# Batch 0's casts, copies and filler matmuls rearranged, and two loads of x split, in a cross-attention and MLP kernel

## The chip, the cores and the metric

One core of one Trainium2 chip. The metric is device time in microseconds (us), median over executions; a profile of one execution gives its span, the time from the first to the last recorded event. The measured time is about 1.8 us above the span of the same execution (213.31 and 211.5 for the profiled run of before).

## The reference, cut to what matters

```python
# x: (8, 8, 512, 64), state: (8, 8, 32, 64), w_in: (512, 2048), w_out: (2048, 512), float32
scores = 0.125 * x @ state.T                # per batch and head: 512 x 32
xread  = softmax(scores) @ state            # 512 x 64
scores2 = 0.125 * state @ x.T
sread  = softmax(scores2) @ x               # 32 x 64
h = concat([xread, sread]) as (4352, 512) @ w_in
out = (h * sigmoid(h)) @ w_out              # (4352, 512)
```

## The kernel before

The kernel multiplies state by w_in beforehand (the tile `W`, one per batch), so that softmax weights times `W` give `h` directly. Almost all of the time goes to two groups of full-width matmuls: G1 (`h`, from softmax weights and `W`) and G2 (`o`, from the activated `h` and w_out). Only batch 0 has nothing to hide behind; its softmax has to be made while the weights are still being loaded. The start, cut:

```python
# loads: x of batch 0 on SyncE in two halves; weights on GpSimd, in this order
load_w_in(0, 128); load_w_in(128, 384)
load_w_out(0, 2);  load_w_out(2, 2)
# ... state of batch 1
load_w_in(512)                              # third piece, columns 512 to 1023
load_w_out(4, 4)
# first half of x (heads 0-3): cast, transpose on TensorE, copy out of PSUM
cast_x(0, nc.vector, 0, 2, 0, 4)            # pieces c = 0, 1
cast_x(0, nc.scalar, 2, 2, 0, 4)            # pieces c = 2, 3
# ...
cast_x(0, nc.scalar, 2, 2, 4, 4)            # second half of x on three engines
cast_x(0, nc.gpsimd, 0, 1, 4, 4)
pe_transpose_x(0, 0, 2, new_o, (nc.vector, nc.vector))
cast_x(0, nc.vector, 1, 1, 4, 4)
# ... (keep_busy(n) is n filler matmuls on zeros)
scores(0, 0); exps(0, 0)
keep_busy(1, psH, "h1")
pe_transpose_x(0, 1, 2, new_h, both)
norm(0, 0)                                  # product on GpSimd
scores(0, 1, 2); exps(0, 1)
norm(0, 1, ((nc.vector, 0, 4),), 2)         # product on VectorE
w1_cols(0, [(0, 128)], (nc.scalar, nc.scalar))
# ... more loads
keep_busy(3, psH, "h1")
pss0 = w1_mms(0, [(128, 384)])              # needs the second piece of w_in
keep_busy(2, psH, "h1")
# attention-weight transposes (first half of heads, then second), their copies,
# G1 for ft = 0..3, G2 for ft = 0, 1, then
# w1_mms(0, [(512, 512)])                   # needs the third piece of w_in
```

In the profile before, every group of matmuls from there on has its inputs in time. Batches 4 to 7 load x on SyncE, 1 MB each, two batches ahead of the one that is being multiplied.

The softmax here doesn't subtract the row's maximum and nothing guards it: scores larger than these inputs give would overflow.

## Time and profile before

| | before |
|---|---|
| time, median of the first 3 runs | 212.74 us |
| its profiled execution | 213.31 us, span 211.5 us |
| TensorE busy | 96% of the span |
| 384-column group starts | 10.29 us, at the landing of its weights |
| 512-column group starts | 15.59 us, at the landing of its weights |
| from there to the end | 195.95 us |

A row of a timeline has the start, the length, engine, source line, operation, output and inputs, shape, count, and in brackets the idle time before it and who ended it. L469 is the multiplication of state by w_in (first a group of 128 columns, then 384, then 512), L398 the attention-weight transposes, L253 the transposes of x, L306 the scores, L165 filler, L525 is G1 and L566 G2. The chain of waits is the path that ended last: start, length, what.

### The profile page before, as it was taken

The numbers are of one execution on the slowest core, as the hardware profiler recorded it, in microseconds if no ns is written. First come the engines' busy times: TensorE is split into PE (matmuls) and PEld (weight loads), VectorE is DVE, ScalarE is ACT, GpSimd is POOL, SyncE is SP. The second block draws the span as 40 slices with busy tenths as digits, with TensorE's granted clock in tenths as the row PEclk, the third lists the DMA queues.
The fourth block names the chain that finished last, engine by engine and source line by source line (L and its number), as shares of the span: only waits on it lengthen the run. The fifth ranks groups of instructions, "written<-read, shape, count | busy, mean of one in ns | idle before, by whom it ended". The sixth has DMA issues, their size and how long they took to land.

```text
span 211.5 us, 3841 instructions
## 1 busy us (share of the span) xinstructions
PE 203.7 (96%) x1550; PEld 96.8 (46%) x1575; DVE 74.1 (35%) x146; ACT 139.3 (66%) x244; POOL 40.1 (19%) x62
## 2 busy tenths in 40 slices
PE   7799999999999999999999999999999999999993
PEld 2444454444444444444444444444444444466653
DVE  3842257657841236113410653043412306100011
ACT  3866677899577867697569855996775166644410
POOL 8672215503320042012201202000200000000000
PEclk9999999999999999999999999999999999999999
DMA  6999999995549756555935429114221111011112
GB/s 196 193 203 207 287 258 340 226 272 179 103 104 239 205 130 138 122 176 102 233 80 183 104 64 207 50 53 99 80 69 37 63 64 53 0 50 50 53 50 99
DMA packets 42929, 28.65 MB, mean 135 GB/s; under 512 B 28064, under 2 KB 37792, under 8 KB 42912
## 3 DMA queue, kind: packets, MB, share of 16 engines
q1 hardware_dynamic: 36720, 20.65, 37.4%
q0 software_dynamic: 5904, 7.64, 17.4%
q8 instruction: 12, 0.20, 0.4%
q10 hardware_dynamic: 288, 0.13, 0.2%
q14 instruction: 5, 0.04, 0.1%
HBM read 17.43 MB, written 8.91 MB: 125 GB/s over the span
## 4 chain that ended last, share of the span: by engine, by line
PE 90%; DMA 5%; POOL 2%; issue 1%; DVE 0%; POOLq 0%
PE o L566 50%; PE h L525 25%; DMA w_in_sb<-in_moe_w_in_dram 5%; PE ps_w L469 4%; PE h L546 3%; PE o_a L566 3%; PE o_part L588 2%; PE ps_sr L416 1%; PE ps_scT L332 1%; POOL w_in_sb L150 1%; POOL w_out_sb L153 1%; PE ps_sc L306 0%; PE ps_xt L253 0%; DVE W L159 0%; POOL st_n L191 0%
## 5 line engine op out<-in xcount | busy, mean ns | idle before, releaser
L566 PE MATMUL o<-w_out_sb,g 128*128 128x512 bf16 x480 | 129.5, 379 | 1.3 <-issue 0.5
L557 ACT ACTIVATE g<-h 128x512 bf16<-128x512 f32 (+1 forms) x143 | 81.3, 573 | 34.1 <-PE h L525 19.9
L566 PEld LDWEIGHTS <-g 128*128 128x128 bf16 x528 | 50.3, 98 | 59.1 <-issue 3.8
L525 PE MATMUL h<-aT,W 128*128 128x512 bf16 x247 | 73.1, 379 | 0.1
L159 DVE COPY o_sb<-o 128x512 f32<-128x512 f32 x15 | 10.4, 691 | 89.1 <-PE o L566 86.2
L525 PEld LDWEIGHTS <-W 128*128 128x128 bf16 x254 | 24.5, 98 | 30.3 <-issue 0.7
L159 DVE CAST W<-ps_w 128x512 bf16<-128x512 f32 (+2 forms) x36 | 22.2, 658 | 23.2 <-PE ps_w L469 23.2
L157 ACT ACTIVATE W<-ps_w 128x512 bf16<-128x512 f32 (+1 forms) x32 | 16.2, 562 | 11.1 <-PE ps_w L469 11.1
L159 POOL CAST x_nat<-x_f 128x512 bf16<-128x512 f32 x24 | 14.7, 655 | 35.7 <-DMA x_f<-in_x_dram 35.7
L157 ACT ACTIVATE o_sb<-o 128x512 f32<-128x512 f32 x16 | 9.5, 597 | 14.4 <-PE o L566 11.9
L362 POOL TENSOR_TENSOR an<-e,rcn 128x512 bf16<-128x512 bf16 x5 | 7.6, 1517 | 48.0 <-DVE rcn L360 48.0
L469 PE MATMUL ps_w<-w_in_sb,stT 64*32 64x512 bf16 (+2 forms) x264 | 10.3, 373 | 0.6 <-DMA w_in_sb<-in_moe_w_in_dram 0.6
L566 PE MATMUL o_a<-w_out_sb,g 128*128 128x512 bf16 x31 | 9.8, 379 | 0.2
L546 PE MATMUL h<-xmT,w_in_sb 128*128 128x256 bf16 x64 | 9.6, 273 | 0.1
L546 PEld LDWEIGHTS <-w_in_sb 128*128 128x128 bf16 x64 | 6.3, 98 | 3.9
L359 DVE TENSOR_REDUCE rs<-e 128x32 f32<-128x1024 bf16 x5 | 6.1, 1213 | 3.1 <-DMA e<-eT 3.1
L165 PE MATMUL ps_busy<-busy 128*128 128x512 bf16 x15 | 5.9, 497 | 1.2 <-DVE warm L172 1.2
L346 ACT ACTIVATE eT<-ps_scT 128x512 bf16<-128x512 f32 x10 | 5.4, 597 | 1.6 <-PE ps_scT L332 1.6
L786 ACT ACT_TABLE_LOAD x5 | 6.4, 1283 | 0.1
L469 PEld LDWEIGHTS <-stT 64*32 64x32 bf16 x264 | 3.2, 90 | 6.0 <-issue 4.1
L382 POOL TENSOR_TENSOR an<-exp_nat,rc 128x512 bf16<-128x512 bf16 x3 | 3.1, 1048 | 14.8 <-DVE rc L380 14.8
L768 ACT ACT_TABLE_LOAD x4 | 5.1, 1283 | 0.1
(76 smaller groups left out, 99.7 us busy)
## 6 DMA issues: line engine op xcount, KB each, us to landing
out_dram<-o_sb SPq DMA_DIRECT2D x33, 256.0 KB, 2.5
x_f<-in_x_dram SPq DMA_DIRECT2D x4, 1024.0 KB, 6.1
x_f<-in_x_dram POOLq DMA_DIRECT2D x2, 1024.0 KB, 11.9
w_in_sb<-in_moe_w_in_dram POOLq DMA_DIRECT2D x3, 512.0 KB, 10.5
x_f<-in_x_dram SPq DMA_DIRECT2D x2, 512.0 KB, 4.7
w_out_sb<-in_moe_w_out_dram POOLq DMA_DIRECT2D x4, 256.0 KB, 12.0
w_out_sb<-in_moe_w_out_dram POOLq DMA_DIRECT2D x2, 512.0 KB, 12.2
x_f<-in_x_dram POOLq DMA_DIRECT2D x2, 512.0 KB, 15.2
```

Of the source, the lines that this page charges most:

```text
L157: nc.scalar.activation(dst, src, func=COPY, bias=0.0)
L159: eng.tensor_copy(dst, src)
L165: nc.tensor.matmul(ps[:], busy[:, 0:128], busy[:], start=True, stop=True, skip_group_check=True)
L346: nc.scalar.activation(t[:, hg], scT_ps[hg][:], func=EXP, bias=0.0, scale=SCALE)
L359: nc.vector.tensor_reduce(rs[:], e2[b][:], axis=AX, op=ADD)
L362: eng.tensor_tensor(a[:, hg], e2[b][:, hg], rc[:, hg].to_broadcast([128, 4, 4, NS]), op=MULT)
L469: nc.tensor.matmul(pss[f, hg][ds(32 * s, 32), 0:n], stT[ds(r, 64), b, h // 2, s % 2, :], w_in_sb[ds(r, 64), h // 2, ds(f, n)], start=True, ...
L525: nc.tensor.matmul(h_ps[k][:], W1[b][:, hg, ds(128 * ft, 128)], aT[b][:, hg, :, :], start=(hg == 0), stop=(hg == 1), skip_group_check=True,)
L546: nc.tensor.matmul(ps[:, 0:256], w_in_sb[:, kt, ds(128 * ft, 128)], xmT[:, :, kt].rearrange("p t n b -> p t (n b)"), start=(kt == 0), stop ...
L557: nc.scalar.activation(g[:, 0:n], ps[:, 0:n], func=SILU, bias=0.0)
L566: nc.tensor.matmul(outs[tt][:], gt[b * NFT + ft][:, ds(128 * tt, 128)], w_out_sb[:, ft, :], start=(ft == 0), stop=(ft == NFT - 1), skip_gr ...
L786: nc.scalar.activation(warm[:], busy[:, 0:1], func=SILU, bias=0.0)
```

## The change

The intent: shorten the path from x to the first G1 by spreading casts and copies and by moving filler matmuls out of it, and make two later loads of x finer. The diff:

```diff
--- before.py
+++ after.py
@@ -257,7 +257,8 @@
                     )
             copy(engs[u], xT[b][:, ds(m * u, m), ds(2 * hg, 2), :], ps[:])
 
-    cast_x(0, nc.vector, 0, 2, 0, 4)
+    for c in (0, 1):
+        cast_x(0, nc.vector, c, 1, 0, 4)
     cast_x(0, nc.scalar, 2, 2, 0, 4)
     for u in range(2):
         copy(
@@ -267,10 +268,9 @@
         )
     o_tags = ["o0", "o1"]
     new_o = lambda sh, dt, nm: psO.tile(sh, dt, tag=o_tags.pop(), name=nm)
-    cast_x(0, nc.scalar, 2, 2, 4, 4)
-    cast_x(0, nc.gpsimd, 0, 1, 4, 4)
-    pe_transpose_x(0, 0, 2, new_o, (nc.vector, nc.vector))
-    cast_x(0, nc.vector, 1, 1, 4, 4)
+    pe_transpose_x(0, 0, 2, new_o, both)
+    for c in (0, 2):
+        cast_x(0, nc.vector, c, 2, 4, 4)
 
     st_x = pers.tile([128, 8, B, 4, 2, 2], BF16)
 
@@ -611,7 +611,6 @@
     keep_busy(1, psH, "h1")
     scores(0, 0)
     exps(0, 0)
-    keep_busy(1, psH, "h1")
     pe_transpose_x(0, 1, 2, new_h, both)
     norm(0, 0)
     scores(0, 1, 2)
@@ -630,11 +629,10 @@
     load_x(2)
     for i in (1, 2):
         ones_beside_x(i, nc.gpsimd)
-    keep_busy(3, psH, "h1")
+    keep_busy(5, psH, "h1")
     banks[:] = ["a2", "a3"]
     turn[0] = 0
     pss0 = w1_mms(0, [(128, 384)])
-    keep_busy(2, psH, "h1")
     for c in (0, 2):
         ps_a = (psO, psA)[c // 2].tile(
             [128, 2, 128], BF16, tag=("o1", "a0")[c // 2], name="ps_at"
@@ -768,7 +766,8 @@
                     nc.scalar.activation(warm[:], busy[:, 0:1], func=EXP, bias=0.0)
                 if m + 1 < B:
                     if at == (0, 2):
-                        load_x(m + 1, eng=nc.sync)
+                        for h in range(0, H, 4 if b < 3 else H):
+                            load_x(m + 1, h, 4 if b < 3 else H, nc.sync)
                     if at == (1, 0):
                         for c in range(4):
                             cast_x(m + 1, nc.gpsimd, c, 1)
```

Casts, copies and filler belong to batch 0; the last hunk splits the loads of batches 4 and 5 in halves of four heads.

## The prediction

> **What bounds the kernel now.** I read the page first (busy shares, slices), then the chain of work that ended last in order of time, then the timelines of TensorE, VectorE and ScalarE over the first 18 us, because every part of the change but one lies there.
>
> The page of the kernel before:
>
> ```profile
> span 211.5 us, 3841 instructions
> PE 203.7 (96%) x1550; PEld 96.8 (46%) x1575; DVE 74.1 (35%) x146; ACT 139.3 (66%) x244; POOL 40.1 (19%) x62
> ```
>
> TensorE is busy 96% of the time; the page's row of slices (5.3 us each) is thin only in the first two and the last. So a gain can come only from matmuls that go away or from the holes at the start. The change removes one matmul, and that one is filler. The chain of waits (columns: start, length, what) says which event the start hangs on:
>
> ```profile
> 1.61 1.63 POOL w_in_sb L150 x2
> ...
> 5.13 10.42 DMA w_in_sb<-in_moe_w_in_dram
> 15.55 0.04 issue
> 15.59 0.62 PE ps_w L469 x16
> ```
>
> Followed back from the end, everything is TensorE to 15.59 us; there the chain leaves TensorE for a transfer, the third piece of the weights w_in (512 columns), issued by GpSimd at 5.13 and landed at 15.55. Ahead of it stand only GpSimd's earlier issues. The casts, transposes and softmax of batch 0, which the change rearranges, are not on this chain at all. The TensorE timeline over the same stretch (start, length, line, operation, count, idle before and who ended it):
>
> ```profile
> 5.54 0.62 PE L253 MATMUL ps_xt<-ident,x_rows 128*128 128x128 bf16 x8 [0.45 <-DVE x_rows L159]
> 6.46 0.62 PE L306 MATMUL ps_sc<-stT,xT 128*128 128x64 bf16 x8
> 6.92 0.38 PE L165 MATMUL ps_busy<-busy 128*128 128x512 bf16 x1
> 7.13 0.67 PE L253 MATMUL ps_xt<-ident,x_rows 128*128 128x128 bf16 x8
> ...
> 10.29 0.36 PE L469 MATMUL ps_w<-w_in_sb,stT 64*32 64x384 bf16 x8 [0.57 <-DMA w_in_sb<-in_moe_w_in_dram]
> 10.57 0.60 PE L165 MATMUL ps_busy<-busy 128*128 128x512 bf16 x2
> 11.02 0.61 PE L398 MATMUL ps_at<-ident,an 128*128 128x128 bf16 x8
> ...
> 14.74 0.81 PE L566 MATMUL o_a<-w_out_sb,g 128*128 128x512 bf16 x3
> 15.59 0.62 PE L469 MATMUL ps_w<-w_in_sb,stT 64*32 64x512 bf16 x16
> ```
>
> There are two gates, and both are weights landing. At 10.29 the second piece of w_in (384 columns) ends a wait of 0.57 us; at 15.59 the third piece arrives just as TensorE gets there. How close it is: the three matmuls from 14.74 start 0.216 us apart (0.81 less the 0.38 of one, over two), the pace of full-width matmuls here, so the slot after them opens at 15.39. At the next group of this kind the trace has a matmul starting at 21.12 and the group at 21.43, 0.09 us more than the pace; with that it would start at about 15.48. It starts at 15.59, so about 0.11 us of it is waiting for the transfer. The two sides are balanced to a tenth of a microsecond.
>
> **What the Trainium skill says.** "TensorE: Matmul & The Clock Gate", section "What's actually happening": the array runs at half clock until it has been busy for a window of about 3.4 us, and falls back after an idle one. The trace agrees: the first seven filler matmuls take 0.43 us each, those after about 4.5 us are spaced 0.22. The change leaves no hole near 3.4 us, so I expect no loss of clock. "ScalarE: Activation LUTs", section "What ACT_TABLE_LOAD costs": an activation with immediate operands costs 186 ns plus 0.833 ns per element, 0.61 us for 512. The trace has 0.60 for that shape, against VectorE's 0.42 for the same bf16 copy out of PSUM; handing the copy to ScalarE is slower by itself and pays only by running beside the other. "SBUF — State Buffer", section "SBUF: two separate sides": a float32 copy on VectorE can lock GpSimd out of the port it needs to write descriptors. This bears on rival B; no row of the trace of before shows such a stall. "DMA: Bandwidth & Descriptors", section "Anatomy of one DMA": about 2.0 us fixed plus a part that scales with size, so splitting a load buys nothing by itself. The page of before agrees in kind: 512 KB of x landed in 4.7 us and 1024 KB in 6.1.
>
> **The change part by part.** VectorE and ScalarE of the kernel before, the rows that move:
>
> ```profile
> 5.06 0.43 DVE L159 CAST x_rows<-x_f 128x512 bf16<-128x512 f32 x1 [1.08 <-DMA x_f<-in_x_dram]
> 5.98 0.75 DVE L159 COPY xT<-ps_xt 128x512 bf16<-128x512 bf16 x2 [0.30 <-PE ps_xt L253]
> 6.65 0.58 DVE L159 CAST x_rows<-x_f 128x256 bf16<-128x256 f32 x1
> 9.98 0.70 DVE L382 TENSOR_TENSOR an<-exp_nat,rc 128x512 bf16<-128x512 bf16 x1
> ...
> 6.45 0.63 ACT L157 ACTIVATE x_rows<-x_f 128x512 bf16<-128x512 f32 x1 [0.47 <-DMA x_f<-in_x_dram]
> 7.84 0.60 ACT L157 ACTIVATE xT<-ps_xt 128x512 bf16<-128x512 bf16 x1
> ```
>
> 1. First cast in two pieces of 256 columns. A cast of 512 takes 0.43 and the next VectorE row starts 0.35 after it, so I estimate a piece to be done 0.28 after its start and the second to start 0.20 later: pieces at 5.34 and 5.54 instead of one at 5.49. TensorE can start its transposes at 5.39 instead of 5.54, but the last four still need ScalarE's cast (5.05 + 0.63 = 5.68). They end 0.05 us earlier.
>
> 2. The two copies out of PSUM: before, VectorE one after the other, 5.98 to 6.73. After: VectorE the first, about 5.9 to 6.3; ScalarE the second from about 6.12, 0.60 long, to 6.72. The scores of the last columns need the second: 6.72 against 6.73, no gain. Those of the first start about 0.1 earlier, which helps nobody, for the exponential waits for all eight.
>
> 3. Second half of x: before, three engines cast it at once (ScalarE 0.63 from 6.45, to 7.08; GpSimd and VectorE about 6.6 to 7.1 and 6.9). After, VectorE alone, two casts of 512 columns from about 6.47: done at 6.90 and 6.47 + 0.35 + 0.43 = 7.25. The last piece comes 0.17 later than before. The filler matmul ahead of these transposes (6.92, 0.21 us of TensorE) goes, so the first four can run at about 7.0 and the last four at 7.29, ending 0.1 earlier than now (7.70 against 7.80). ScalarE's copy then starts at 7.74 instead of 7.84, and all of the softmax after it comes 0.1 earlier: VectorE's last product ends at 10.58 instead of 10.68, GpSimd's half at 10.03 instead of 10.13.
>
> 4. Filler matmuls: five ahead of the 384-column group instead of three ahead and two behind. The two ahead cost nothing, for TensorE waits there until 10.29 in any case (two take 0.43, the wait is 0.57). With the two behind gone, the transposes of the attention weights start at 10.57 instead of 11.02, and both halves are ready (10.03, and 10.58 for the half wanted from 10.80). Gain at this point: 0.45 us, the only real one of the change, and everything up to the second gate moves by it.
>
> 5. The second gate. TensorE now reaches the 512-column group at 15.48 - 0.45 = 15.03. The transfer lands at 15.55 as before: GpSimd issues it at 5.13, ahead of the cast that it loses, and its packets queue behind those of five earlier transfers of the same queue. TensorE waits 0.5 us instead of 0.1, and starts at 15.59. Gain kept: 0.00.
>
> 6. The two loads of x (batches 4 and 5, issued near 44.5 and 66.3 us) become two halves each: two more issues of about 0.45 us on SyncE. Their readers are casts on GpSimd, which for each piece need all heads, so no reader starts earlier; and TensorE waits for nothing after 15.59 that the waits view lists beyond tenths of a microsecond. Off the path: 0.00.
>
> Sum: start of the unbroken part at 15.59, its length 211.5 - 15.59 = 195.9 us unchanged, span 211.5; the measured time is 1.24 us above the span (212.74 against 211.5). Predicted 212.7 us.
>
> **The rivals.** A, the gain goes through: if the 512-column transfer landed earlier, or were not the gate, 0.45 us would reach the end, giving 212.3. For it: the filler is plainly on TensorE's order, and GpSimd loses a cast of 0.47 us. Against: that cast follows the issue of the transfer, and the queue is full from 5.13 on. B, VectorE's longer float32 casts (about 0.75 us from 6.5 instead of 0.28) hold back GpSimd's descriptors, the weights land later, and the end moves by up to that 0.5 us: 213.2. Against: the third piece's issue is over at 5.93, before those casts. C, VectorE, now with both halves of the cast, becomes the bound of the softmax: it would have to lose more than 0.55 us against my count to show at 15.59. Nothing like that is in sight, so 212.7 still. D, the split loads shift completions in the SyncE queue and a later transpose comes too late: the casts of batch 4 start at 51.85 without waiting for the load of 44.5, so slack is several microseconds; even a stall of half a microsecond in each of two batches gives 213.7.
>
> **Range and chances.** The main line and C give 212.7, A 212.3, B 213.2; runs of before lie within 0.02 us of each other. Eight in ten: 212.2 to 213.2. Two per cent is 4.25 us; no rival gives a quarter of that. Within 2%: 0.98; the rest is split evenly between what I have overlooked on either side.
>
> **What would show it.** In the profile after: the attention-weight transposes start near 10.57 with no filler ahead of them; TensorE's idle time before the 512-column group grows to about 0.5 us, named after the transfer, which lands at 15.5 to 15.6; that group starts within 0.1 of 15.59; the chain still leaves TensorE there; busy TensorE falls by about 0.2 us. I am wrong in step 5 if that group starts by 15.2, in step 3 if the attention-weight transposes start after 11.0, in step 6 if TensorE gets a new wait between 44 and 80 us.

## The result, and the profile after

212.65 us (212.49 to 212.92, six runs), against 212.84 us (212.74 to 213.74, six runs) of the kernel before. The ratio is 0.9986, 95% interval 0.9968 to 1.0003: the same within 2%, inside the range. A ratio is the mean time of one kernel's fast runs over that of the other's of the same rounds, so not quite the ratio of the medians quoted.

The page of the kernel after:

```profile
span 211.1 us, 3867 instructions
PE 206.0 (98%) x1574; PEld 97.3 (46%) x1574; DVE 74.0 (35%) x147; ACT 139.1 (66%) x244; POOL 39.1 (19%) x61
```

The span is 0.4 us shorter than that of the profile before. The rise of busy TensorE is no work: the program has one matmul fewer, while the trace has 24 more records (1574 against 1550), because more of them were lost in the profile before. The chain of waits of the kernel after, over the stretch where that of before stood on a transfer:

```profile
7.55 0.60 ACT exp_nat L320
8.15 0.50 ACT xT L157
...
9.16 1.19 PE ps_busy L165 x5
...
10.63 0.33 PE ps_at L398 x4
...
10.96 0.30 PE ps_at L398 x2
...
14.63 0.65 PE o_a L566 x3
15.28 0.59 PE ps_w L469 x16
```

No transfer is in this stretch any more. It passes through the softmax of batch 0 (ScalarE's exponential and copy), then goes along TensorE: the five filler matmuls, the attention-weight transposes, and on without a wait for a transfer into the 512-column group. The timeline of TensorE (rows that answer to those of before):

```profile
4.64 1.03 PE L165 MATMUL ps_busy<-busy 128*128 128x512 bf16 x2
...
7.35 0.61 PE L253 MATMUL ps_xt<-ident,x_rows 128*128 128x128 bf16 x8
...
10.27 0.36 PE L469 MATMUL ps_w<-w_in_sb,stT 64*32 64x384 bf16 x8
10.56 0.80 PE L398 MATMUL ps_at<-ident,an 128*128 128x128 bf16 x8
...
14.47 0.81 PE L566 MATMUL o_a<-w_out_sb,g 128*128 128x512 bf16 x3
15.21 0.66 PE L469 MATMUL ps_w<-w_in_sb,stT 64*32 64x512 bf16 x16
```

The chain goes from one TensorE piece to the next at 10.96. What held the second four transposes there, their weight loads tell:

```profile
10.96 0.23 PEld L398 LDWEIGHTS <-an 128*128 128x128 bf16 x4 [0.17 <-DVE an L382]
```

The transposes started at 10.56 as predicted (10.57), but the predicted wait of 0.5 us for the 512 columns is not there: the third piece landed at 14.80 instead of 15.55, and the group started at 15.21 with no wait named. And the second half of the transposes waited for VectorE's product, which ended at 10.91 where I had 10.58. In the first row two filler matmuls take 1.03 us; in the profile before the row of these two was 4.49 to 5.10, 0.61 long. Two things that the change doesn't touch, the landing of a weight and the pace of the array at 5 us, differ by more than the gain in question. So one profile of each kernel could not say what the change did, and the first task was to repeat them.

### The profile page after: what moved, and what is told of

It reads as the page before. It is cut to its first block, busy times and chain, and to the rows that moved or that the text cites. A ratio compares the mean times of both kernels' runs of the same rounds, so it can differ in the third digit from the quotient of the medians.

```text
span 211.1 us, 3867 instructions
## 1 busy us (share of the span) xinstructions
PE 206.0 (98%) x1574; PEld 97.3 (46%) x1574; DVE 74.0 (35%) x147; ACT 139.1 (66%) x244; POOL 39.1 (19%) x61
## 4 chain that ended last, share of the span: by engine, by line
PE 97%; ACT 1%; DVE 1%; issue 0%
PE o L566 51%; PE h L525 26%; PE ps_w L469 4%; PE h L546 3%; PE o_a L566 3%; PE ps_busy L165 3%; PE o_part L588 2%; PE ps_sr L416 1%; PE ps_xt L253 1%; PE ps_scT L332 1%; PE ps_sc L306 1%; ACT xT L157 1%; PE ps_at L398 1%; DVE W L159 0%; ACT exp_nat L320 0%; PE h L507 0%
## 5 line engine op out<-in xcount | busy, mean ns | idle before, releaser
L566 PE MATMUL o<-w_out_sb,g 128*128 128x512 bf16 x496 | 132.0, 379 | 0.0
L525 PE MATMUL h<-aT,W 128*128 128x512 bf16 x254 | 74.6, 379 | 0.1
L159 POOL CAST x_nat<-x_f 128x512 bf16<-128x512 f32 x24 | 14.2, 631 | 34.4 <-issue 22.3
```

What stands on the lines that cost most here:

```text
L159: eng.tensor_copy(dst, src)
L525: nc.tensor.matmul(h_ps[k][:], W1[b][:, hg, ds(128 * ft, 128)], aT[b][:, hg, :, :], start=(hg == 0), stop=(hg == 1), skip_group_check=True,)
L566: nc.tensor.matmul(outs[tt][:], gt[b * NFT + ft][:, ds(128 * tt, 128)], w_out_sb[:, ft, :], start=(ft == 0), stop=(ft == NFT - 1), skip_gr ...
```

## The experiments

Twelve kernels ran, in three sets of four; each set shared a chip and the runs of the kernel before. All were correct. The table sums up what their profiles show. "Full pace from" is when the trace's clock record, which no view prints, says that the array left half clock (no record in one); "product" the end of VectorE's last softmax product; "transposes" the start of the second four attention-weight transposes; "landing" the last of the 16 engines of the third w_in piece; "group" the start of the 512-column group; "rest" from there to the end.

| kernel | full pace from | product | transposes | landing | group | rest | span |
|---|---|---|---|---|---|---|---|
| before, first profile | 4.17 | 10.67 | 11.24 | 15.55 | 15.59 | 195.95 | 211.5 |
| after, first profile | 6.74 | 10.91 | 10.96 | 14.80 | 15.21 | 195.94 | 211.1 |
| e1 before again | 6.61 | 11.06 | 11.12 | 15.19 | 15.37 | 195.97 | 211.3 |
| e2 after again | none | 10.58 | 10.63 | 15.07 | 15.12 | 195.84 | 211.0 |
| e3 filler only | 6.75 | 10.73 | 10.79 | 14.58 | 15.04 | 195.97 | 211.0 |
| e4 casts only | 5.32 | 10.65 | 10.71 | 14.97 | 15.01 | 196.17 | 211.2 |
| e5 before, piece earlier | 7.02 | 10.95 | 11.00 | 13.38 | 15.25 | 195.98 | 211.2 |
| e6 after, piece earlier | 6.20 | 10.81 | 10.87 | 13.66 | 15.11 | 195.87 | 211.0 |
| e7 after, piece later | 5.04 | 10.57 | 10.63 | 18.19 | 18.23 | 197.45 | 215.7 |
| e8 loads only | 5.01 | 10.68 | 10.74 | 14.75 | 14.99 | 195.86 | 210.8 |
| e9 filler only, piece earlier | 7.00 | 10.79 | 10.85 | 13.32 | 15.10 | 196.00 | 211.1 |
| e10 after, piece half later | 4.12 | 11.26 | 11.32 | 15.90 | 15.94 | 195.81 | 211.8 |
| e11 before, 384 late | 7.12 | 10.92 | 11.53 | 14.55 | 15.77 | 195.98 | 211.7 |
| e12 after, 384 late | 6.32 | 10.86 | 11.09 | 14.58 | 15.33 | 195.86 | 211.2 |

All fourteen obey one rule within 0.02 us: the group starts at the later of transposes + 4.25 us and landing + 0.05 us. The 4.25 us are TensorE's own work between the two. I formed the rule on the first six profiles; the eight after them test it.

The clock records show one thing more. In all thirteen profiles that have one, the array stayed at full clock for a whole number of times 3.413 us: 60 or 61 of them, and in e7 four, then one at half clock, then 57. So in these executions the clock changed only on a grid of that step, which lay differently in each; full pace starting anywhere between 4.12 and 7.12 us, a range of 3.0 us, fits that.

**e1, the kernel before again.** No edit; five rounds.

> The kernel before, unchanged, a second time, to learn what one profile is worth. The first profile had the third piece of w_in landing at 15.55 us, and the last of the 16 engines of that transfer 1.86 us behind the first; the profile of the changed kernel had 14.80 and 1.20 us. Theory G (the landing is the gate, as I predicted): the landing is a property of the queue, it comes at 15.5 to 15.6 again and the 512-column group starts at 15.6, span 211.5. Theory S (the lag of the last engines differs from run to run, and apart from it the softmax chain of batch 0 sets the start): landing anywhere from 14.7 to 15.6, and where it is below 15.0 the group starts 4.2 to 4.3 us after the second half of the attention-weight transposes, at 15.2 or earlier; span = 195.9 + that start, near 211.0. Time against the kernel before: ratio 1.000 in both.

Measured: 212.94 us, ratio 0.9995 (0.9971 to 1.0019). TensorE:

```profile
4.64 1.03 PE L165 MATMUL ps_busy<-busy 128*128 128x512 bf16 x2
...
10.04 0.36 PE L469 MATMUL ps_w<-w_in_sb,stT 64*32 64x384 bf16 x8
10.33 0.61 PE L165 MATMUL ps_busy<-busy 128*128 128x512 bf16 x2
10.77 0.75 PE L398 MATMUL ps_at<-ident,an 128*128 128x128 bf16 x8
...
15.37 0.66 PE L469 MATMUL ps_w<-w_in_sb,stT 64*32 64x512 bf16 x16
```

The same program, a different limit: neither the 384-column group nor the 512-column group waits for a transfer, and the group starts 4.25 us after the second half of the transposes (11.12). Here the softmax, delayed by the slow start of the array, sets everything. Theory G is out for this execution. The sixteen engines of the first w_in transfer finished between 5.99 and 7.91 us, as wide a spread as in the first profile (6.24 to 8.26).

**e2, the changed kernel again.** No edit; five rounds.

> The changed kernel, unchanged, a second time. Its first profile had TensorE still at half pace until about 6.3 us and the 512-column group at 15.21 without a wait for the transfer. Theory G: landing 14.8 is what the change does (one cast fewer on GpSimd), so it is at 14.7 to 14.9 again. Theory S: the landing is again anywhere from 14.7 to 15.6; if below 14.9, the group starts 4.2 to 4.3 us after the second half of the attention-weight transposes, at 14.9 to 15.2. Span 210.7 to 211.1. Ratio to the kernel before 0.998 to 1.000 in both.

Measured: 212.82 us, ratio 0.9991 (0.9966 to 1.0016), with the array early at full pace (the two fillers at 4.64 took 0.71 us). The row of the 512-column group:

```profile
15.12 0.62 PE L469 MATMUL ps_w<-w_in_sb,stT 64*32 64x512 bf16 x16 [0.16 <-DMA w_in_sb<-in_moe_w_in_dram]
```

Now the transfer binds after all: transposes at 10.63 would have let the group start at 14.88, the landing was 15.07. By this count it cost 0.24 us; the 0.16 of the row is smaller because it counts from the modelled end of the matmul before. So the landing is not fixed at 14.8 by the change either.

**e3, the filler alone.** Two fillers from behind the 384-column group to ahead of it, and the one between scores and transposes gone:

```diff
     exps(0, 0)
-    keep_busy(1, psH, "h1")
     pe_transpose_x(0, 1, 2, new_h, both)
...
-    keep_busy(3, psH, "h1")
+    keep_busy(5, psH, "h1")
     pss0 = w1_mms(0, [(128, 384)])
-    keep_busy(2, psH, "h1")
```

> The kernel before with the change of the filler matmuls alone (one gone between scores and transposes, two moved from behind the 384-column group to ahead of it); casts and copies stay as before. My step 4: the attention-weight transposes begin right behind the 384-column group, the second half of them waits for VectorE's product (ended 10.68 in the first profile of before), so they start at about 10.7 instead of 11.25 and the 512-column group at about 14.95 if the transfer lets it, else at its landing. So this part alone carries the whole gain of the change: ratio 0.998 to 0.999. If the filler is worth nothing, because TensorE was waiting for the softmax anyway, the second half starts no earlier than in the repeat of before, and the ratio is 1.000.

Measured: 212.79 us, ratio 0.9992 (0.9967 to 1.0017), above the expected 0.998 to 0.999. Product at 10.73, transposes at 10.79, group at 15.04. Against before in the same late-pace start (11.06, 10.95 and 10.92 in e1, e5 and e11) the product comes 0.25 us earlier than their mean. Some 0.1 us of that is the execution's own: its first transposes of x began at 5.50, against a mean of 5.59 in those three. Counted from there the product takes 5.23 us, here and in e9, against 5.38 to 5.39 in those three: 0.15 us. The two moved fillers took no part: the transposes followed the product by 0.06. What is left of the edit ahead of the product is the removed filler, before the second transposes of x; that one counts.

**e4, the casts and copies alone.**

```diff
-    cast_x(0, nc.vector, 0, 2, 0, 4)
+    for c in (0, 1):
+        cast_x(0, nc.vector, c, 1, 0, 4)
...
-    cast_x(0, nc.scalar, 2, 2, 4, 4)
-    cast_x(0, nc.gpsimd, 0, 1, 4, 4)
-    pe_transpose_x(0, 0, 2, new_o, (nc.vector, nc.vector))
-    cast_x(0, nc.vector, 1, 1, 4, 4)
+    pe_transpose_x(0, 0, 2, new_o, both)
+    for c in (0, 2):
+        cast_x(0, nc.vector, c, 2, 4, 4)
```

> The kernel before with the change of casts and copies alone (first cast in two pieces, ScalarE copies half of the first transposes, VectorE casts the whole second half of x, none on GpSimd); filler and loads stay. My step 3 gave the end of VectorE's last product 0.1 us earlier with the filler gone; here the filler matmul ahead of the second transposes stays, so at best 0.0, and the profile of the changed kernel even showed it 0.23 later (10.91 against 10.68). Expected: product ends at 10.6 to 10.9, ratio 1.000 to 1.001. Theory G's rider (the GpSimd cast holds descriptors back): lag of the last engine of the first w_in transfer 0.7 us as in the changed kernel, against 2.0 in the first profile of before, and landing of the third piece at 14.8. Theory S: lag as it falls.

Measured: 212.85 us, ratio 0.9995 (0.9972 to 1.0019). The product ended at 10.65, against 10.67 and 10.68 for before with an early pace (first profile and e8): nothing gained, as expected. The rest took 196.17 us here, 0.2 more than elsewhere, and the trace says why: a third gate. The third transfer of w_out (512 KB, issued at 5.87) landed at 18.34, and the G2 matmul that follows started at 18.39, 0.43 us after the one before it instead of 0.216. In the first profile after the same transfer landed at 18.44 and cost 0.07 us. The rider on GpSimd's cast is not supported: the first w_in transfer's last engine came 0.78 us after the first here, but 0.87 in e3, 0.87 in e5 and 0.71 in e8, all of which have that cast. Spreads of 2 us occurred in two of seven profiles with the cast (the first of before and e1) and in none of seven without it, too few to tell.

**e5 and e6, the third piece one place earlier,** in the kernel before and in the changed one:

```diff
     load_w_out(0, 2)
-    load_w_out(2, 2)
     # ... state of batch 1
     load_w_in(512)
+    load_w_out(2, 2)
     load_w_out(4, 4)
```

> The kernel before with the third piece of w_in (512 columns) issued one place earlier: ahead of the second 256 KB of w_out, which it swaps places with. From six profiles: the 512-column group starts at the later of (second half of attention-weight transposes + 4.25 us) and (landing of the third piece + 0.05). The swap should bring the landing about 1.2 us earlier, to 13.4 to 14.3, so the second bound falls away. If my reading is right the group starts exactly 4.25 us after the transposes, with no wait for the transfer: 15.3 to 15.5, span 211.2 to 211.4, ratio 0.999 to 1.000. If the landing alone is the gate (theory G) the group starts near 14.3 and the ratio is 0.994.

> The same swap in the changed kernel. Reading of the two bounds: group 4.25 us after the second half of the attention-weight transposes, which follow VectorE's last product (ended 10.58 and 10.91 in two profiles), so 14.9 to 15.2, span 210.8 to 211.1, ratio to the kernel before 0.998 to 0.999, at most 0.2 us better than the changed kernel without the swap. Theory G: group near 14.3, ratio 0.994. Against the run above it gives the worth of the change with the transfer out of the way: 0.1 to 0.4 us, so that the landing took away less than I predicted.

Measured: e5 212.94 us, ratio 1.0002 (0.9990 to 1.0015); e6 212.75 us, ratio 0.9994 (0.9981 to 1.0008), both a little above the expected ratios. The landing went to 13.38 and 13.66, and the group started at 15.25 and 15.11, 4.25 and 4.24 us after the transposes. With the transfer wholly out of the way nothing is won, so theory G (group near 14.3) is out. With both starts late, the difference of the two kernels is 0.14 us in the group's start and 0.2 us in the medians.

**e7, the third piece one place later,** behind 512 KB of w_out, in the changed kernel:

```diff
-    load_w_in(512)
     load_w_out(4, 4)
+    load_w_in(512)
```

> The changed kernel with the third piece of w_in issued one place later, behind 512 KB of w_out: a control that must bind. Landing about 2.5 us later, 17.1 to 18.0; the 512-column group starts 0.05 after it and the end moves by as much: span 213.0 to 214.0, ratio 1.010 to 1.014, TensorE's wait for the transfer about 2 us. If anything else hides it (the order of TensorE, a later slack), the ratio stays below 1.005.

Measured: 217.25 us, ratio 1.0193 (1.0166 to 1.0220), unclear at 2%: more than I expected. TensorE's row of the group, and what the windows view has for the stretch behind it (length, busy time and count of each engine, then the granted clock, the transfer share and GB/s):

```profile
18.23 0.67 PE L469 MATMUL ps_w<-w_in_sb,stT 64*32 64x512 bf16 x16 [3.28 <-DMA w_in_sb<-in_moe_w_in_dram]
18.83 1.04 PE L566 MATMUL o<-w_out_sb,g 128*128 128x512 bf16 x2
```

```profile
18.20:21.80 3.60, 3.57 (x24) 1.19 (x24) 1.29 (x2) 1.28 (x3) 1.60 (x3) 0.57 1.24 205
```

The gate binds: landing 18.19, group 18.23. The surprise is the second cost. After 3.28 us of idling the array ran at half clock from 18.69 to 22.10 us by the clock record, with full-width matmuls 0.427 us apart instead of 0.216, and the rest took 197.45 us instead of 195.84 (e2). Against the 14.88 at which the transposes would have let the group go and that rest, the span is 5.0 us longer for a wait of 3.28. One of the four runs took 215.93 us, 1.6 less than the profiled one. It left no trace, but its granted clock is on record: 1.0, against 0.992 in the three others, and 3.41 us at half clock in a span of 215.7 make 0.992. So it was spared the half clock, though it waited about as long: its span of 214.1 less the rest of 195.84 puts its group at an estimated 18.3. The length of the idle time alone does not decide, then. That fits the grid above: in the profiled run the half clock came 0.46 us after the group had started, at the fourth step from 5.04. The Trainium skill, "TensorE: Matmul & The Clock Gate", section "HAM oscillation — how this bites in real kernels", has the rule as no idle gaps above about 3.4 us; I had applied it to the change, and not to my own control.

**e8, the split loads alone.**

```diff
-                        load_x(m + 1, eng=nc.sync)
+                        for h in range(0, H, 4 if b < 3 else H):
+                            load_x(m + 1, h, 4 if b < 3 else H, nc.sync)
```

> The kernel before with the two loads of x split and nothing else. My step 6: off the path, ratio 1.000, the stretch from the 512-column group to the end 195.9 to 196.0 us as in five of six profiles, GpSimd's casts of batches 4 and 5 no earlier than before (51.9 and 73.7 less the shift of the start). If the split makes a later transfer late (rival D), that stretch grows by 0.3 us or more; if it relieves something, it shrinks by as much.

Measured: 212.64 us, ratio 0.9993 (0.9980 to 1.0005); rest 195.86 us. On TensorE's path nothing moved, as predicted. The readers' start proved a poor witness: GpSimd's casts of batch 5 start at 71.36 us here, against 73.70 in the first profile of before, but at 71.07 to 72.28 in five others with the load in one piece (e1, e3, e4, e5, e9). But the rest is shorter. With the loads split it is 195.81 to 195.87 us (e2, e6, e8, e10, e12, and first after less its 0.07), with the loads in one piece 195.95 to 196.00 (six profiles, and e4 less its wait). The difference lies behind the last matmul: from the landing of the last store to the end of the span are 0.90 to 0.93 us in the seven profiles with the split, and 1.03 to 1.05 in the seven without. At the end SyncE goes through nine semaphore waits in a fixed order, 0.065 us apart when all has landed. Without the split, the last store's landing releases the seventh, and two more follow; with the two additional loads it releases the ninth. So the split shortens the end by 0.1 us through the place of one semaphore in that list, and not through its loads. The rest of this kernel's low median I put down to its head, that of the kernel before in an early-pace start without the late landing; one profile doesn't show that for five runs.

**e9, the version that these runs pointed to:** filler alone (e3) and the piece earlier (e5).

> The version that the runs so far point to: the kernel before with the filler change alone and the third piece of w_in issued one place earlier. In the half-pace start the filler change alone had VectorE's last product at 10.73 us, against 11.06 and 10.95 for the kernel before and 10.91 and 10.81 for the whole change; the swap keeps the landing out of the way. Expected: product at 10.4 to 10.75, 512-column group 4.25 us after the second half of the attention-weight transposes, 14.75 to 15.05, span 210.6 to 211.0, ratio 0.998 to 0.9995. If the whole change is needed after all, it comes out at 1.000 like the kernel before.

Measured: 212.88 us, ratio 1.0001 (0.9987 to 1.0014). Product 10.79, just outside what I expected, group 15.10, span 211.1. It beats neither kernel. The 0.1 us of head that it has in hand over the whole change in late starts (10.73 and 10.79 against 10.91, 10.81 and 10.86) doesn't show in the time; the shorter end of the split loads, which this kernel lacks (rest 196.00 against 195.87 in e6), is as large.

**e10, the third piece behind 256 KB,** in the changed kernel:

```diff
-    load_w_in(512)
-    load_w_out(4, 4)
+    load_w_out(4, 2)
+    load_w_in(512)
+    load_w_out(6, 2)
```

> The changed kernel with the third piece of w_in issued behind 256 KB of w_out (half of what stood ahead of it in the late control, where a wait of 3.28 us was followed by matmuls at half pace, the stretch from the group to the end growing from 195.9 to 197.4 us). Landing near 16.2, wait about 1 to 1.5 us. If the half pace came from the length of the idle time, it does not come here: the stretch stays 195.9 to 196.0, span 212.1 to 212.4, ratio 1.004 to 1.008. If any wait at this place brings it, the stretch is 197 again and the ratio 1.012 or more.

Measured: 213.63 us, ratio 1.0037 (1.0023 to 1.0050), a little under the expected range. The rule holds: landing 15.90, group 15.94, rest 195.81 with no half pace. But the wait was 0.31 us and not 1 to 1.5, because this execution's softmax was late as well (the first transposes of x, which wait for the first casts, began at 5.70 us, and the product ended at 11.26). So it shows that a wait of 0.3 us brings no half clock, and leaves open where between 0.3 and 3.3 us it begins.

**e11 and e12, the 384 columns late,** in the kernel before and in the changed one:

```diff
-    load_w_in(128, 384)
     load_w_out(0, 2)
+    load_w_in(128, 384)
```

> The kernel before with the second piece of w_in (384 columns) swapped with the first 256 KB of w_out, so that it lands about 1.2 us later, at 10.4 to 11.0, as late as or later than in the first profile of before (10.24). My step 4 in the case where it applies: TensorE starts the 384-column group at the landing, then 0.28 for it and 0.45 for the two fillers, then 0.22 for the first transposes: second half of the attention-weight transposes 0.95 us after the group's start, at 11.4 to 11.9, later than VectorE's product; 512-column group 4.25 later, 15.65 to 16.2; span 211.6 to 212.1, ratio 1.002 to 1.005. If the softmax chain still sets it, the transposes follow the product by 0.05 and the ratio is 1.000.

> The same swap in the changed kernel, whose two fillers stand ahead of the group and are over by then. Second half of the transposes 0.50 us after the 384-column group's start, so with the same landing 0.45 us earlier than in the run above: 10.9 to 11.5; 512-column group at 15.2 to 15.7; span 211.1 to 211.6. Difference to the run above 0.45 us (0.3 to 0.5), which is my step 4 at full size. If the filler is worth nothing here either, the two runs lie within 0.15 us.

Measured: e11 213.52 us, ratio 1.0031 (1.0018 to 1.0043); e12 212.94 us, ratio 1.0002 (0.9990 to 1.0015). TensorE of e11:

```profile
10.57 0.35 PE L469 MATMUL ps_w<-w_in_sb,stT 64*32 64x384 bf16 x8 [0.61 <-DMA w_in_sb<-in_moe_w_in_dram]
10.86 0.61 PE L165 MATMUL ps_busy<-busy 128*128 128x512 bf16 x2
11.30 0.61 PE L398 MATMUL ps_at<-ident,an 128*128 128x128 bf16 x8
...
15.77 0.66 PE L469 MATMUL ps_w<-w_in_sb,stT 64*32 64x512 bf16 x16
```

and of e12:

```profile
10.57 0.36 PE L469 MATMUL ps_w<-w_in_sb,stT 64*32 64x384 bf16 x8 [0.26 <-DMA w_in_sb<-in_moe_w_in_dram]
10.86 0.62 PE L398 MATMUL ps_at<-ident,an 128*128 128x128 bf16 x8
...
15.33 0.66 PE L469 MATMUL ps_w<-w_in_sb,stT 64*32 64x512 bf16 x16
```

In both the 384 columns let TensorE go at 10.57; then before runs its two fillers and the changed kernel does not. 15.77 less 15.33 is 0.44 us, and it reaches the end: the spans are 0.56 us apart (medians 0.58), and the other 0.12 is the shorter end that e8 showed. This is my step 4 at full size, with the cause held fixed, and the kernel in which the moved fillers are worth having.

## Why the prediction was right or wrong

The time was right: 212.7 against 212.65, in the range. That was partly luck: step 4 had too large a gain and step 5 too large a loss, and the two cancelled; and the base was one slow execution, whose error the sum took back when it added too little to the span.

- **The reading of before.** I took one profile for the kernel. Its execution was slow, 213.31 us against a median of 212.74, and I added the 1.24 us between its span and that median as if it were an overhead; within one execution the difference is 1.8. What made it slow was the last engine of the w_in transfers: 384 columns at 10.24, 512 at 15.55. In the other profiles with the loads in their original order these two landed at 9.28 to 9.88 and 14.58 to 15.19. The transfer is a gate in some executions (first profile, e2, e4), the softmax in the others, and the two lie within 0.5 us.
- **Steps 1 and 2** hold in an early-pace start: e2's ScalarE copied from 6.14, where I had 6.12. With a late pace the second copy ended at 7.17 instead of 6.72 in the first profile after, and the product comes at 10.86 in the mean of three, against 10.76 in e3 and e9, which keep the old casts and copies: there they cost 0.1 us.
- **Step 3** was right: I put VectorE's last product at 10.58 after 10.68. Like with like, 10.58 and 10.57 (e2, e7) stand against 10.67 and 10.68 (first profile, e8) with an early pace, and a mean of 10.86 against 10.98 with a late one (after, e6, e12 against e1, e5, e11). (e10 has an early pace too and is left out: VectorE's first cast of x started at 5.35 there, against 4.96 in e2.) The 0.1 us comes from the one removed filler (e3) and not from the casts (e4).
- **Step 4 was mis-sized:** 0.45 us for the fillers moved ahead. It assumed the 384 columns at 10.28. Landing at 9.2 to 9.9, they leave room for the two fillers before the product is ready, and the transposes follow the product by 0.05 to 0.06 in both kernels. The worth is about 0.1 us, that of step 3. With the landing held late it is 0.44 (e11, e12).
- **Step 5 failed in its mechanism:** I had the second gate swallow the whole gain, with a wait of 0.5 us. Measured: no wait in the first profile after, 0.16 us in e2 (0.24 by the rule); and with the gate removed (e5, e6) the gain was 0.14 us, not 0.45. There was little to swallow.
- **Step 6** was right about the readers and about TensorE (e8), and wrong in its 0.00: the two additional loads shorten the end of the program by 0.1 us, which no step had. The section on DMA that the prediction cites for it describes transfers issued from GpSimd, while these loads are issued from SyncE; the 4.7 and 6.1 us of the page are SyncE's.
- **The rivals.** A, a gain that goes through, is what happens, at 0.1 to 0.15 us at the head instead of 0.45. B, descriptors held back by VectorE's casts, is not seen: the landings of the changed kernel in its original order, 14.80 and 15.07, lie within those of the kernel before. C and D are not seen.

Head and end together make about 0.2 us. Whether the time itself fell is less sure than that: the ratios 0.9986 and 0.9991 have intervals that hold 1.000, the medians differ by 0.19 us in the first comparison and by 0.02 in e2's, and without one run of before, 213.74 us, the first ratio would be 0.9993.

## What to carry to other kernels

Before building on a wait, look whether a second profile has it: here the gate that one profile named in every view was gone in the next one of the same program, and differences below the spread of landings (1 us) and of the array's warm-up had to be compared like with like. Where two chains meet within some tenths of a microsecond, write down when each would let the next step go; a rule of two terms gave the group's start in fourteen profiles, and each term could be moved by itself by reordering the loads. Filler matmuls are free ahead of a wait; behind one they can cost their full length (e11 against e12). Look behind the last matmul too: a change in the number of transfers moved the end by as much as the softmax moved the start (e8).

## What the Trainium skill lacked or had wrong

- "TensorE: Matmul & The Clock Gate", section "What you observe", has the rise to full clock about 4 us into sustained work, plus or minus 0.5. Here the filler begins at 1.19 us in every profile, and full clock came at 4.12 to 7.12 us, 2.9 to 5.9 us later. That moved the softmax of batch 0 by 0.3 us. The granted-clock column did not show the half pace at the start (1.00 in the stretch 4.5 to 6.5 us of the first profile after, where two full-width matmuls took 1.03 us); the spacing of the rows did.
- The same page, "HAM oscillation — how this bites in real kernels": a gap just short of its figure, 3.28 us idle, was followed by half clock, which then lasted 3.41 us (e7); another run of the same kernel, with about the same wait by its span, kept full clock.
- "DMA: Bandwidth & Descriptors", section "Latency and other measured facts", says that certain engines are usually slower. It has no figure for how far the 16 engines of one load lie apart: here 0.6 to 2.0 us for the first w_in transfer, differing from one execution of the same program to the next, and a wait ends only with the last.
